# Gradient of single-query attention: the next pair's K scores moved ahead of its V transposes

## The chip, the cores and the metric

The kernel runs on one core of a Trainium2 chip. The metric is device time in microseconds (us); lower is better. The core has a TensorE (PE in the profile) for matmuls, a VectorE (DVE), a ScalarE (ACT), a GpSimd (POOL, used here only to set constants up) and a SyncE (SP), which here issues nearly all transfers between the main memory and the on-chip buffers. Each engine works its own instructions in order and waits on semaphores for the others.

## The reference

The forward pass is attention with one query per head over 8192 keys, 32 heads, 128 wide, in bf16; the outputs are its result and the gradients with respect to q, k and v for a given gradient of the output.

```python
B, H, Sq, Skv, Dh = 1, 32, 1, 8192, 128
def _fwd_reference(q, k, v):
    scale = q.shape[-1] ** -0.5
    scores = jnp.einsum('bhqd,bhkd->bhqk', q, k) * scale
    attn = _softmax(scores, axis=-1)
    return jnp.einsum('bhqk,bhkd->bhqd', attn, v)
_out, _vjp = jax.vjp(_f, q, k, v)
_grads = _vjp(grad_out)
return (_out0, *grads)          # out, dq, dk, dv
```

Per head this is: s = K q, p = softmax(scale s), out = V^T p, dp = V do, ds = scale p (dp - sum(p dp)), dq = K^T ds, dk = ds q^T, dv = p do^T. K and V are read once (134 MB), dk and dv, of the same size, are written once; all else is small.

## The kernel before

**Tiles.** Two heads make a pair; there are 16 pairs (HP). K and V of a pair are tiles of 128 partitions by 128 rows by 128 columns, 4 MB each. There are three K buffers and two V buffers, taken from pools whose tiles go round: a load of pair t takes the buffer that K of pair t-3, or V of pair t-2, leaves. dK is written into K's own buffer and dV into V's, eight blocks of 16 rows each, and stored from there; so a buffer is free for its next load when its store has landed.

**Steps of a pair t**, by function:
- `k_block(t, c)`, c from 0 to 7: VectorE transposes a block of K in 32x32 squares (L184, tile XK_sb, three buffers); TensorE multiplies it by a window on q (four matmuls, L192) into the bank s_ps.
- `s_back`, `s_top`, `s_exp`, `s_sum`, `p_of`: the softmax. VectorE turns s_ps back (L199) and takes the maximum (L204), TensorE turns it over partitions (L207), VectorE reduces (L214), ScalarE takes the exponential (L217), TensorE sums (L222), VectorE inverts (L233), ScalarE writes p (L235) and the window win_p (L228).
- `v_bank(t, m)` and `v_copy(t, m)`, m from 0 to 15: TensorE transposes four squares of V into one of three PSUM banks (L249), ScalarE copies the bank to XV_sb (L255). `v_scores(t, z)` multiplies four such banks by do (L266) into dp_ps. A bank can be refilled only after its copy.
- `contract(t, "p")`: out from V, 32 matmuls (L305); `contract(t, "ds")`: dq from K, 32 matmuls. `gather`, every fourth pair, brings their sums out (L312, L317, L319).
- `v_back`, `pd_sum`, `ds_of`: VectorE turns dp back (L276), the products' sum goes over TensorE (L285), VectorE makes ds (L290, L292, L295), ScalarE the window win_ds.
- `outer(t, "p", r)` and `outer(t, "ds", r)`, r from 0 to 7: VectorE writes dV over V and dK over K, a block at a time (L325). `store` issues the transfer on SP (L335), `load` the loads (L80).

**Order.** It is written out by hand (`tc.manual_schedule`), one list for all engines; each engine takes its own instructions in the order of that list. The body for pair t holds also the dK blocks of the pair before, o = t-1, in pieces (`dk(a, b)`). On VectorE the order is: eight K blocks of t, dK block 0 of o, the softmax of t between dK blocks 1 to 7, dpT, dV block 0, ds, dV blocks 1 to 7. On TensorE `early(t+1)`, which is banks 0 to 8 and score group 0 of the next pair's V, stands right behind `contract(t, "ds")` and `prepare(t+1)`, thus ahead of the next pair's K matmuls. ScalarE copies these nine banks while VectorE writes dV. On SP the order per pair is: store of dK of o (behind its block 7), store of dV of t, load of K of t+2, load of V of t+2. SP waits in that order, too: for VectorE before a store, for the old store's landing before a load.

**Beginning and end.** At the start K of pair 0 is loaded in quarters, then V(0), K(1), V(1), K(2). V(0)'s gradient is stored in quarters, and V(2) is then loaded in quarters. The last pair's dV and dK are stored in quarters, and dK of pair 14 in halves.

Of the kernel before, what the change touches and what calls it, by code (L numbers as in the profile page):

```python
# [11 lines left out]
BF16 = mybir.dt.bfloat16  # L12
# [3 lines left out]
NB = 8  # L16
# [6 lines left out]
K_BUFS = 3  # L23
V_BUFS = 2
# [3 lines left out]
def kernel(  # L28
# [12 lines left out]
    P = 128  # L41
    _, H, S, D = k.shape
    HP = H // 2
    NT = 2 * S // P
# [9 lines left out]


    consts = ctx.enter_context(tc.tile_pool(name="consts", bufs=1))
    kpool = ctx.enter_context(tc.tile_pool(name="kp", bufs=K_BUFS))
    vpool = ctx.enter_context(tc.tile_pool(name="vp", bufs=V_BUFS))
    xkpool = ctx.enter_context(tc.tile_pool(name="xkp", bufs=3))
    xvpool = ctx.enter_context(tc.tile_pool(name="xvp", bufs=2))  # L60
    backs = ctx.enter_context(tc.tile_pool(name="backs", bufs=2))
# [6 lines left out]
    psQ = ctx.enter_context(tc.tile_pool(name="psQ", bufs=1, space=PSUM))  # L68
    psM = ctx.enter_context(tc.tile_pool(name="psM", bufs=1, space=PSUM))

    Kt, Vt, st, acc = {}, {}, {}, {}

    def rows_of(x, t, a, b):
        return x[0, 2 * t:2 * t + 2].rearrange("h s d -> (h s) d").rearrange("(p n) d -> p n d", p=P)[:, a:b, :]

    def load(x, X, t, pool, tag, parts):
        X[t] = pool.tile([P, NT, D], BF16, tag=tag, name=tag + "t")
        L = NT // parts
        for c in range(parts):
            nc.sync.dma_start(X[t][:, c * L:(c + 1) * L, :], rows_of(x, t, c * L, (c + 1) * L))  # L80

    def load_k(t, parts=1):
        load(k, Kt, t, kpool, "K", parts)

    def load_v(t, parts=1):
        load(v, Vt, t, vpool, "V", parts)

    rows = consts.tile([H, 2, D], BF16)
    nc.sync.dma_start(rows[:, 0, :], q.rearrange("b h s d -> (b h s) d"))
# [1 line left out]
    load_k(0, 4)  # L91
    load_v(0)
    load_k(1)
    load_v(1)
    load_k(2)

    ident = consts.tile([P, P], BF16)
# [74 lines left out]
    def weights_q(t):  # L172
        nc.scalar.copy(q_win[:].rearrange("p c (a j) -> p c a j", j=SL)[:, :, 0:P // SL, SL - 1].rearrange(  # L173
            "p c (a j) -> p c a j", a=NQ)[:, :, :, 0], q_blk[:, t])

    def weights_do(t):
        for z in range(2):
            nc.scalar.copy(do_win[z * W:(z + 1) * W, :, :, SL - 2 + z].rearrange("p s e -> p e s"),
                           do_cols[z * W:(z + 1) * W, :, 2 * t:2 * t + 2])

    def k_block(t, c):
        x = st[t]
        X = xkpool.tile([P, BN, NW, QD], F32, tag="XK", name="XK_sb")
        nc.vector.transpose(X[:], Kt[t][:, c * BN:(c + 1) * BN, :].rearrange("p n d -> p (n d)").bitcast(F32).rearrange(  # L184
            "p (n w j) -> p n w j", n=BN, w=NW))
        if c == 0:
            x["s"] = psS.tile([P, 512], F32, tag="s", name="s_ps")
        cols = X[:].rearrange("p n w i -> p (n w i)").bitcast(BF16).rearrange(
            "p (n w i e) -> p w e n i", n=BN, w=NW, e=2)
        for w in range(NW):  # L190
            for e2 in range(2):
                nc.tensor.matmul(x["s"][:], lhsT=q_win[:, 2 * w + e2, SL - 1 - c:SL - 1 - c + P],  # L192
                                 rhs=cols[:, w, e2], start=(c == 0 and w == 0 and e2 == 0),
                                 stop=(c == NB - 1 and w == NW - 1 and e2 == 1), skip_group_check=True)

    def s_back(t):
        x = st[t]
        x["sT"] = backs.tile([P, BN, QD], F32, tag="back", name="sT")
        nc.vector.transpose(x["sT"][:].rearrange("p n r -> p (n r)"), x.pop("s")[:])  # L199
# [21 lines left out]
    def s_sum(t, rs):  # L221
        nc.tensor.matmul(st[t]["m"][:, 0:1], lhsT=same[:], rhs=rs[:], start=True, stop=True, skip_group_check=True)  # L222
# [17 lines left out]
    def v_bank(t, m):  # L240
        x = st[t]
        z, i = divmod(m, NM // TB)
        if i == 0:
            x["XV", z] = xvpool.tile([P, NM, P], F32, tag="XV", name="XV_sb")
        T_ps = psT.tile([P, TB, P], F32, tag="T", name="T_ps")
        words = Vt[t][:].rearrange("p n d -> p (n d)").bitcast(F32)
        for j in range(TB):
            at = (i * TB + j) * NZ + z
            nc.tensor.transpose(T_ps[:, j, :], words[:, at * P:(at + 1) * P], ident_f[:])  # L249
        x["T", m] = T_ps  # L250

    def v_copy(t, m):
        x = st[t]
        z, i = divmod(m, NM // TB)
        nc.scalar.copy(x["XV", z][:, i * TB:(i + 1) * TB, :], x.pop(("T", m))[:])  # L255

    def v_scores(t, z):
        x = st[t]
        cols = x.pop(("XV", z))[:].rearrange("p m s -> p (m s)").bitcast(BF16).rearrange(
            "p (m s e) -> p e m s", s=P, e=2)  # L260
        if z == 0:
            x["dp"] = psD.tile([P, 512], F32, tag="dp", name="dp_ps")
        at = SL - 2 - 2 * z
        for e2 in range(2):
            for b in range(NQ):
                nc.tensor.matmul(x["dp"][b * QD:(b + 1) * QD, :], lhsT=do_win[:, b // 2, e2, at:at + QD],  # L266
                                 rhs=cols[:, e2, :, b * QD:(b + 1) * QD],
                                 start=(z == 0 and e2 == 0), stop=(z == NZ - 1 and e2 == 1), skip_group_check=True)
# [62 lines left out]
    def store(t, which, parts=1, last=None):  # L331
        X, dst = (Kt[t], out_2) if which == "ds" else (Vt[t], out_3)
        L = NT // parts
        for c in (range(parts) if last is None else (last,)):
            nc.sync.dma_start(rows_of(dst, t, c * L, (c + 1) * L), X[:, c * L:(c + 1) * L, :])  # L335
# [9 lines left out]

    NV = NZ * NM // TB

    EARLY = 9

    def early(t):  # L350
        for m in range(EARLY):
            v_bank(t, m)
            v_copy(t, m)
            if m == 5:
                v_scores(t, 0)

    q_columns()
    do_columns()
    prepare(0)
    weights_q(0)  # L360
    weights_do(0)
    for t in range(HP + 1):
        o = t - 1
        now, old = t < HP, t > 0

        parts = 4 if o == HP - 1 else 2 if o == HP - 2 else 1

        def dk(a, b):
            for r in range(a, b if old else a):
                outer(o, "ds", r)  # L370
                if (r + 1) % (NB // parts) == 0:
                    store(o, "ds", parts, r * parts // NB)

        if now:
            for c in range(NB):
                k_block(t, c)
            if t + 1 < HP:
                weights_q(t + 1)
        dk(0, 1)
        if now:  # L380
            if old:
                v_scores(t, 1)
                v_bank(t, 9)
                v_copy(t, 9)
            s_back(t)
            s_top(t)
        dk(1, 2)
        if now:
            rs = s_exp(t)
            if old:  # L390
                for m in (10, 11, 12):
                    v_bank(t, m)
            s_sum(t, rs)
            if old:
                v_copy(t, 10)
                v_copy(t, 11)
        dk(2, 3)
        if now:
            p_of(t)
            if old:  # L400
                v_copy(t, 12)
                v_bank(t, 13)
                v_copy(t, 13)
                contract(t, "p")
                v_bank(t, 14)
                v_copy(t, 14)
                v_scores(t, 2)
                v_bank(t, 15)
                v_copy(t, 15)
                v_scores(t, 3)  # L410
            else:
                for m in range(NV):
                    v_bank(t, m)
                    v_copy(t, m)
                    if m == 7:
                        contract(t, "p")
                    if m % 4 == 1 and m > 1:
                        v_scores(t, m // 4 - 1)
                v_scores(t, 3)
            if t + 1 < HP:  # L420
                weights_do(t + 1)
        dk(3, NB)
        if not now:
            break
        v_back(t)
        pd_sum(t)
        if t % ST == ST - 1:
            gather(t, "p")
        if t % ST == 0 and old:
            gather(o, "ds")  # L430
        outer(t, "p", 0)
        ds_of(t)
        contract(t, "ds")
        if t + 1 < HP:
            prepare(t + 1)
            early(t + 1)
        else:
            gather(t, "ds")
            result(o_all, out_0)
            result(dq_all, out_1)  # L440
        fine = t == 0 or t == HP - 1
        for r in range(1, NB):
            outer(t, "p", r)
            if fine and r % 2:
                store(t, "p", 4, r // 2)
        if not fine:
            store(t, "p")
        if 0 < t and t + 2 < HP:
            load_k(t + 2)
        if t + 2 < HP:  # L450
            load_v(t + 2, 4 if t == 0 else 1)
# [32 lines left out]
```

## Time and profile before

| | |
|---|---|
| Time, median of 3 runs | 648.37 us (647.52 to 649.14) |
| The profiled execution: its time | 647.27 us |
| its span, first to last instruction | 645.5 us |
| TensorE matmuls busy | 445.6 us (69%) |
| VectorE busy | 505.0 us (78%) |
| ScalarE busy | 203.8 us (32%) |
| Moved by DMA | 268.97 MB, mean 417 GB/s |
| Mean granted TensorE clock | 0.831 |
| VectorE waits for the K matmuls (L184, on s_ps) | 82.0 us |
| TensorE waits for V loads (L249) | 80.3 us in 14 waits |
| ScalarE waits for V transposes (L255) | 179.0 us |

Busy time is the time in which an engine had an instruction under way; waiting, and the issuing of transfers, is not counted. A wait is put down to what ended it. Transfers are in flight long after they were issued: the page gives 19.4 us from issue to landing for a V tile of 4 MB and 23.8 us for the store of a dK tile. Busy shares are means over the whole span; what holds the end up must be read stage by stage.

### The profile page before, as it was taken

What the parts mean: (1) busy time and instruction counts of PE and PEld (TensorE: products, weight loads), DVE (VectorE), ACT (ScalarE), POOL (GpSimd) and SP (SyncE); (2) the same over time, 40 slices, a digit from 0 to 9 for tenths busy, and PEclk for the clock granted to TensorE, in tenths of its full rate; (3) what the DMA queues carried; (4) which work ended last, traced back from release to release, by engine and by line L of the source; (5) the groups of instructions that cost most, each with busy time, mean ns of one, the idle gap of its engine ahead of it and who ended that gap; (6) DMA issues with size and microseconds to landing.
All of it is one profiled execution on the core that took longest, in us unless ns stands there. A gap on an engine that the chain in (4) does not pass through costs nothing.

```text
span 645.5 us, 7988 instructions
## 1 busy us (share of the span) xinstructions
PE 445.6 (69%) x3256; PEld 252.8 (39%) x3256; DVE 505.0 (78%) x608; ACT 203.8 (32%) x456; POOL 4.4 (1%) x10
## 2 busy tenths in 40 slices
PE   5678795585967758577684965849667586765860
PEld 2444342443535334254442634425353342533430
DVE  8169899498796888858789696986959878597885
ACT  1443333332343323134232333313334142342320
POOL 2000000000000000000000000000000000000000
PEclk9789798686887869878698887869869696796985
DMA  8998999999999999999999999999999999999589
GB/s 358 446 429 330 354 421 435 434 425 437 429 429 428 434 428 425 432 437 423 432 437 429 430 434 427 429 441 427 423 439 424 420 434 422 438 422 423 249 376 374
DMA packets 11748, 268.97 MB, mean 417 GB/s; under 512 B 1472, under 2 KB 1472, under 8 KB 1472
## 3 DMA queue, kind: packets, MB, share of 16 engines
q1 hardware_dynamic: 11568, 268.45, 97.6%
q8 instruction: 25, 0.41, 0.2%
q14 instruction: 11, 0.09, 0.0%
q10 hardware_dynamic: 144, 0.02, 0.0%
HBM read 134.23 MB, written 134.23 MB: 416 GB/s over the span
## 4 chain that ended last, share of the span: by engine, by line
DMA 46%; DVE 24%; PE 18%; issue 5%; ACT 4%; SPq 0%; DVEq 0%; ACTq 0%
DMA Vt<-in_v_dram 25%; DMA out_dram<-Vt 22%; DVE Vt L325 12%; PE T_ps L249 10%; DVE XK_sb L184 4%; PE acc_p L305 4%; DVE Kt L325 3%; PE dp_ps L266 2%; ACT XV_sb L255 2%; DVE dpT L276 1%; PE s_ps L192 1%; ACT p_rep L235 1%; DVE sT L199 1%; ACT win_p L228 1%; PE m_ps L317 1%
## 5 line engine op out<-in xcount | busy, mean ns | idle before, releaser
L249 PE MATMUL T_ps<-ident_f,Vt 128*128 128x128 f32 x1024 | 167.6, 322 | 81.4 <-DMA Vt<-in_v_dram 80.3
L184 DVE STREAM_TRANSPOSE XK_sb<-Kt 128x1024 f32<-128x1024 f32 x128 | 147.6, 1210 | 82.2 <-PE s_ps L192 82.0
L255 ACT COPY XV_sb<-T_ps 128x512 f32<-128x512 f32 x256 | 141.0, 588 | 179.7 <-PE T_ps L249 179.0
L249 PEld LDWEIGHTS T_ps<-ident_f,Vt 128*128 128x128 f32 x1024 | 141.3, 167 | 118.0 <-issue 96.8
L325 DVE TENSOR_TENSOR Kt<-ds_rep,qd 128x2048 bf16<-128x2048 bf16 x128 | 149.9, 1214 | 0.5
L325 DVE TENSOR_TENSOR Vt<-p_rep,qd 128x2048 bf16<-128x2048 bf16 x128 | 148.0, 1217 | 0.0
L192 PE MATMUL s_ps<-XK_sb,q_win 128*128 128x512 bf16 x512 | 124.7, 382 | 7.2 <-DVE XK_sb L184 2.0
L192 PEld LDWEIGHTS <-q_win 128*128 128x128 bf16 x512 | 49.7, 97 | 76.4 <-issue 23.9
L305 PE MATMUL acc_ds<-Kt,win_ds 128*32 128x512 bf16 x512 | 53.2, 590 | 26.4 <-ACT win_ds L228 26.4
L305 PE MATMUL acc_p<-Vt,win_p 128*32 128x512 bf16 x512 | 40.2, 469 | 19.3 <-ACT win_p L228 19.3
L266 PE MATMUL dp_ps<-XV_sb,do_win 128*32 128x512 bf16 x512 | 40.7, 393 | 10.8 <-ACT XV_sb L255 10.8
L276 DVE STREAM_TRANSPOSE dpT<-dp_ps 128x512 f32<-128x512 f32 x16 | 11.5, 717 | 36.9 <-PE dp_ps L266 36.9
L173 ACT COPY q_win<-q_blk 128x16 bf16<-128x16 bf16 x16 | 4.3, 267 | 111.5 <-PE s_ps L192 111.1
L305 PEld LDWEIGHTS <-win_ds 128*32 128x32 bf16 x512 | 17.4, 132 | 50.3 <-ACT win_ds L228 25.8
L305 PEld LDWEIGHTS <-win_p 128*32 128x32 bf16 x512 | 14.2, 110 | 37.9 <-ACT win_p L228 22.8
L170 ACT CAST qd<-m_ps 128x256 bf16<-128x256 f32 x16 | 6.0, 372 | 55.9 <-PE m_ps L166 55.7
L285 PE MATMUL m_ps<-pd,same 128*128 128x1 f32 x32 | 6.5, 273 | 19.4 <-DVE m_ps L279 19.4
L266 PEld LDWEIGHTS <-do_win 128*32 128x32 bf16 x512 | 9.3, 95 | 26.8 <-issue 26.8
L228 ACT COPY win_ds<-ds 64x128 bf16<-64x128 bf16 x32 | 9.5, 296 | 24.9 <-DVE ds L292 24.7
L285 PEld LDWEIGHTS m_ps<-pd,same 128*128 128x128 f32 x32 | 5.2, 203 | 27.3 <-DVE m_ps L279 27.3
L217 ACT ACTIVATE e<-sT,nbias 128x128 f32<-128x128 f32 x16 | 8.2, 512 | 17.5 <-DVE nbias L214 17.5
L199 DVE STREAM_TRANSPOSE sT<-s_ps 128x512 f32<-128x512 f32 x16 | 11.5, 717 | 1.4 <-PE s_ps L192 1.1
(59 smaller groups left out, 141.5 us busy)
## 6 DMA issues: line engine op xcount, KB each, us to landing
Vt<-in_v_dram SPq DMA_DIRECT2D x15, 4096.0 KB, 19.4
Kt<-in_k_dram SPq DMA_DIRECT2D x15, 4096.0 KB, 19.6
out_dram<-Kt SPq DMA_DIRECT2D x14, 4096.0 KB, 23.8
out_dram<-Vt SPq DMA_DIRECT2D x14, 4096.0 KB, 21.5
out_dram<-Vt SPq DMA_DIRECT2D x8, 1024.0 KB, 9.9
Kt<-in_k_dram SPq DMA_DIRECT2D x4, 1024.0 KB, 7.9
Vt<-in_v_dram SPq DMA_DIRECT2D x4, 1024.0 KB, 8.9
out_dram<-Kt SPq DMA_DIRECT2D x2, 2048.0 KB, 8.4
```

What stands on the lines that cost most here:

```text
L184: nc.vector.transpose(X[:], Kt[t][:, c * BN:(c + 1) * BN, :].rearrange("p n d -> p (n d)").bitcast(F32).rearrange("p (n w j) -> p n w j", ...
L192: nc.tensor.matmul(x["s"][:], lhsT=q_win[:, 2 * w + e2, SL - 1 - c:SL - 1 - c + P], rhs=cols[:, w, e2], start=(c == 0 and w == 0 and e2 == 0),
L199: nc.vector.transpose(x["sT"][:].rearrange("p n r -> p (n r)"), x.pop("s")[:])
L217: nc.scalar.activation(e[:].rearrange("p (c n) -> p n c", c=NB), x["sT"][:, :, 0:NB], ACT.Exp, bias=nbias[:], scale=scale, accum_out=rs[:])
L228: nc.scalar.copy(win[which][a:b, :, at + 4 * s:at + 4 * s + 4], src[a:b].rearrange("p (g j) -> p g j", j=4))
L249: nc.tensor.transpose(T_ps[:, j, :], words[:, at * P:(at + 1) * P], ident_f[:])
L255: nc.scalar.copy(x["XV", z][:, i * TB:(i + 1) * TB, :], x.pop(("T", m))[:])
L266: nc.tensor.matmul(x["dp"][b * QD:(b + 1) * QD, :], lhsT=do_win[:, b // 2, e2, at:at + QD], rhs=cols[:, e2, :, b * QD:(b + 1) * QD], start ...
L276: nc.vector.transpose(dpT[:].rearrange("p m r -> p (m r)"), x.pop("dp")[:])
L285: nc.tensor.matmul(x["m"][:, 1:2], lhsT=same[:], rhs=x["pd"][:], start=True, stop=True, skip_group_check=True)
L305: nc.tensor.matmul(acc[which][b * QD:(b + 1) * QD, :], lhsT=win[which][:, g, at:at + QD], rhs=X[:, 4 * g:4 * g + 4, :].rearrange("p n d -> ...
L325: nc.vector.tensor_tensor(X[:, a:b, :].rearrange("p n (a b) -> p n a b", b=R), x[which][:, a:b, :].unsqueeze(2).to_broadcast([P, BN, D // ...
```

## The change

K and V live in fixed buffers (three and two named tiles) instead of pool tiles, used in the same turn; a load waits for what touched the same part of the buffer. The K blocks of pair t+1 move from the start of body t+1 into body t: blocks 0 to 3 stand between dV blocks 3 to 7 of pair t, block 4 behind the last one, and blocks 5, 6 and 7 behind the store of dV, each followed by one V bank of t+1 (0 to 2). Then the window on q for pair t+2 is set. `early` is gone: banks 3 to 15 and the four score groups of a pair stand in its own body, between the dK blocks and the softmax. The K blocks of pair 0 are in the prologue. Loads and stores are the same, in the same order on SP.

```diff
@@ -54,8 +54,6 @@
 
 
     consts = ctx.enter_context(tc.tile_pool(name="consts", bufs=1))
-    kpool = ctx.enter_context(tc.tile_pool(name="kp", bufs=K_BUFS))
-    vpool = ctx.enter_context(tc.tile_pool(name="vp", bufs=V_BUFS))
     xkpool = ctx.enter_context(tc.tile_pool(name="xkp", bufs=3))
     xvpool = ctx.enter_context(tc.tile_pool(name="xvp", bufs=2))
     backs = ctx.enter_context(tc.tile_pool(name="backs", bufs=2))
@@ -68,22 +66,25 @@
     psQ = ctx.enter_context(tc.tile_pool(name="psQ", bufs=1, space=PSUM))
     psM = ctx.enter_context(tc.tile_pool(name="psM", bufs=1, space=PSUM))
 
-    Kt, Vt, st, acc = {}, {}, {}, {}
+    st, acc = {}, {}
+    k_in = [consts.tile([P, NT, D], BF16, name=f"K{i}") for i in range(K_BUFS)]
+    v_in = [consts.tile([P, NT, D], BF16, name=f"V{i}") for i in range(V_BUFS)]
+    Kt = {t: k_in[t % K_BUFS] for t in range(HP)}
+    Vt = {t: v_in[t % V_BUFS] for t in range(HP)}
 
     def rows_of(x, t, a, b):
         return x[0, 2 * t:2 * t + 2].rearrange("h s d -> (h s) d").rearrange("(p n) d -> p n d", p=P)[:, a:b, :]
 
-    def load(x, X, t, pool, tag, parts):
-        X[t] = pool.tile([P, NT, D], BF16, tag=tag, name=tag + "t")
+    def load(x, X, t, parts):
         L = NT // parts
         for c in range(parts):
             nc.sync.dma_start(X[t][:, c * L:(c + 1) * L, :], rows_of(x, t, c * L, (c + 1) * L))
 
     def load_k(t, parts=1):
-        load(k, Kt, t, kpool, "K", parts)
+        load(k, Kt, t, parts)
 
     def load_v(t, parts=1):
-        load(v, Vt, t, vpool, "V", parts)
+        load(v, Vt, t, parts)
 
     rows = consts.tile([H, 2, D], BF16)
     nc.sync.dma_start(rows[:, 0, :], q.rearrange("b h s d -> (b h s) d"))
@@ -345,24 +346,23 @@
 
     NV = NZ * NM // TB
 
-    EARLY = 9
-
-    def early(t):
-        for m in range(EARLY):
-            v_bank(t, m)
-            v_copy(t, m)
-            if m == 5:
-                v_scores(t, 0)
+    def v_part(t, m):
+        v_bank(t, m)
+        v_copy(t, m)
+
+    HALF = NB // 2
 
     q_columns()
     do_columns()
     prepare(0)
     weights_q(0)
     weights_do(0)
+    for c in range(NB):
+        k_block(0, c)
+    weights_q(1)
     for t in range(HP + 1):
         o = t - 1
         now, old = t < HP, t > 0
-
         parts = 4 if o == HP - 1 else 2 if o == HP - 2 else 1
 
         def dk(a, b):
@@ -371,47 +371,45 @@
                 if (r + 1) % (NB // parts) == 0:
                     store(o, "ds", parts, r * parts // NB)
 
-        if now:
-            for c in range(NB):
-                k_block(t, c)
-            if t + 1 < HP:
-                weights_q(t + 1)
-        dk(0, 1)
+        dk(0, 2)
         if now:
             if old:
-                v_scores(t, 1)
-                v_bank(t, 9)
-                v_copy(t, 9)
+                v_part(t, 3)
+                v_part(t, 4)
             s_back(t)
             s_top(t)
-        dk(1, 2)
+            if old:
+                v_scores(t, 0)
+                v_part(t, 5)
+                v_part(t, 6)
+        dk(2, 3)
         if now:
             rs = s_exp(t)
             if old:
-                for m in (10, 11, 12):
+                for m in (7, 8, 9):
                     v_bank(t, m)
             s_sum(t, rs)
             if old:
-                v_copy(t, 10)
-                v_copy(t, 11)
-        dk(2, 3)
+                v_copy(t, 7)
+                v_copy(t, 8)
+        dk(3, 4)
         if now:
             p_of(t)
             if old:
-                v_copy(t, 12)
-                v_bank(t, 13)
-                v_copy(t, 13)
+                v_copy(t, 9)
+                v_scores(t, 1)
+                v_part(t, 10)
+                v_part(t, 11)
                 contract(t, "p")
-                v_bank(t, 14)
-                v_copy(t, 14)
+                v_part(t, 12)
+                v_part(t, 13)
                 v_scores(t, 2)
-                v_bank(t, 15)
-                v_copy(t, 15)
+                v_part(t, 14)
+                v_part(t, 15)
                 v_scores(t, 3)
             else:
                 for m in range(NV):
-                    v_bank(t, m)
-                    v_copy(t, m)
+                    v_part(t, m)
                     if m == 7:
                         contract(t, "p")
                     if m % 4 == 1 and m > 1:
@@ -419,7 +417,7 @@
                 v_scores(t, 3)
             if t + 1 < HP:
                 weights_do(t + 1)
-        dk(3, NB)
+        dk(4, NB)
         if not now:
             break
         v_back(t)
@@ -433,7 +431,6 @@
         contract(t, "ds")
         if t + 1 < HP:
             prepare(t + 1)
-            early(t + 1)
         else:
             gather(t, "ds")
             result(o_all, out_0)
@@ -443,8 +440,16 @@
             outer(t, "p", r)
             if fine and r % 2:
                 store(t, "p", 4, r // 2)
+            if t + 1 < HP and r >= HALF - 1:
+                k_block(t + 1, r - HALF + 1)
         if not fine:
             store(t, "p")
+        if t + 1 < HP:
+            for c in range(HALF + 1, NB):
+                k_block(t + 1, c)
+                v_part(t + 1, c - HALF - 1)
+            if t + 2 < HP:
+                weights_q(t + 2)
         if 0 < t and t + 2 < HP:
             load_k(t + 2)
         if t + 2 < HP:
```

## The prediction

> **What bounds the kernel now.** I read first the sliced page (who is busy when), then long windows of the DMA engines, then the order of issues on SP, then VectorE's timeline in the first pairs. The page's DMA rows:
>
> ```profile
> DMA  8998999999999999999999999999999999999589
> GB/s 358 446 429 330 354 421 435 434 425 437 429 429 428 434 428 425 432 437 423 432 437 429 430 434 427 429 441 427 423 439 424 420 434 422 438 422 423 249 376 374
> q1 hardware_dynamic: 11568, 268.45, 97.6%
> ```
>
> The transfers fill the span except in slices 3 to 4 (48 to 81 us) and 37 (597 to 613 us). The windows (busy time of each engine, clock, DMA share, GB/s) say it closer:
>
> ```profile
> 90.00:590.00 500.00, 349.22 (x2571) 198.46 (x2569) 400.30 (x477) 158.58 (x354) 0.00 (x0) 0.83 1.00 430
> ...
> 62.00:64.00 2.00, 1.52 (x12) 1.04 (x9) 1.82 (x6) 1.52 (x5) 0.00 (x0) 1.00 0.18 74
> 64.00:66.00 2.00, 0.73 (x13) 0.33 (x16) 2.00 (x3) 1.93 (x5) 0.00 (x0) 0.98 0.02 8
> ...
> 608.00:610.00 2.00, 1.52 (x12) 1.13 (x10) 1.84 (x5) 1.45 (x4) 0.00 (x0) 1.00 0.08 33
> 610.00:612.00 2.00, 0.74 (x14) 0.33 (x16) 1.98 (x3) 1.92 (x5) 0.00 (x0) 1.00 0.00 0
> ```
>
> From 90 to 590 us the DMA share is 1.00 at 430 GB/s: no order of the compute can win there, only lose. What can be won are two holes, at 62 to 66 and near 604 to 612 us. The issues on SP show how the transfers queue:
>
> ```profile
> 69.93 0.34 SPq L335 DMA_DIRECT2D out_dram<-Kt  x1
> 83.03 0.34 SPq L335 DMA_DIRECT2D out_dram<-Vt  x1
> 90.22 0.34 SPq L80 DMA_DIRECT2D Kt<-in_k_dram  x1
> 99.91 0.34 SPq L80 DMA_DIRECT2D Vt<-in_v_dram  x1
> ...
> 611.47 4.88 SPq L335 DMA_DIRECT2D out_dram<-Kt  x2
> 622.87 7.14 SPq L335 DMA_DIRECT2D out_dram<-Vt  x4
> ```
>
> The K load at 90.22 waited for K(0)'s store to land, the V load at 99.91 for V(1)'s store: 9.69 us apart, which is one 4 MB tile at 430 GB/s (4.19/0.430 = 9.75). The landings in the trace follow one another by 9.65 to 10.05 us through the span (a few by 10.4 to 11.4): one line, served in order of issue, 9.7 us for a tile, 2.45 to 2.5 us for a quarter. So the time is the sum of transfers plus the moments in which the line is empty. Per pair it is four tiles, 39.3 us (V loads land at 119.95 and 591.28, twelve pairs apart). VectorE has 505.0/16 = 31.6 us of work per pair.
>
> An empty line also costs a start. The page lists K(14)'s two 2 MB stores with 8.4 us to landing, the first of them issued into an empty line, where 2 MB move in 4.85: about 3.4 us. The first quarter of V(2), issued at 65.21 into an empty line, landed at 71.03, 5.8 where 2.5 is the transfer: again 3.4.
>
> VectorE at the first pairs:
>
> ```profile
> 38.44 0.72 DVE L276 STREAM_TRANSPOSE dpT<-dp_ps 128x512 f32<-128x512 f32 x1 [17.34 <-PE dp_ps L266]
> 41.46 8.03 DVE L325 TENSOR_TENSOR Vt<-p_rep,qd 128x2048 bf16<-128x2048 bf16 x7
> 49.41 9.12 DVE L184 STREAM_TRANSPOSE XK_sb<-Kt 128x1024 f32<-128x1024 f32 x8
> 71.95 0.72 DVE L276 STREAM_TRANSPOSE dpT<-dp_ps 128x512 f32<-128x512 f32 x1 [2.05 <-PE dp_ps L266]
> 74.97 8.03 DVE L325 TENSOR_TENSOR Vt<-p_rep,qd 128x2048 bf16<-128x2048 bf16 x7
> ```
>
> A product block (L325) is 8.03/7 = 1.147 us, a K block (L184) 9.12/8 = 1.14, and without a wait for V a pair takes 33.5 us from one dpT to the next (the following one, 71.95 to 103.83, 31.9).
>
> **The change, part by part.** Nothing is removed: 8 K blocks, 16 V banks and 16 product blocks per pair stay, and no DMA is added.
>
> *Quarter release of V(0).* In the changed instruction order each quarter load of V(2) waits for its own quarter's store; before, the first waited for all four (landings 57.8, 60.2, 62.7, 65.1). Back to back the loads would land at 67.6, 70.1, 72.5, 75.0 instead of 71.0, 73.5, 76.0, 80.4 (3.4 us start, and a fourth quarter of 4.4). Quarters 2 and 3 are stored later now (2 and 4 K blocks ahead of them: 47.25+2.3 and 49.52+4.6 = 54.1), still ahead of their turn. Worth up to 5.4 us, if something follows. Elsewhere a tile is loaded whole and waits for one store as before: the fixed buffers cost and give nothing.
>
> *K blocks ahead of the V store.* K blocks 0 to 3 of the next pair (4 x 1.14 = 4.6 us) now stand before the last dV block, and with it before the store of V on SP; behind that store in SP's queue stand the K load, the V load and the dK store.
>
> *V transposes later.* Nine banks and one score group, which ran on TensorE and ScalarE under the dV blocks, now follow the K blocks. Listing the changed order for pair 1 with durations from rows (K block 1.14, product 1.147, four K matmuls 7.91/8 = 0.99, bank 1.53/3 = 0.51, ScalarE copy 0.55, score group 0.58, p contraction 2.5 = 40.2/16, from 0.47 and 0.59 for the softmax steps): the last K block ends on VectorE at 58.0 (before 58.5), its matmuls at 59.7; banks 2 to 4 to 61.3; the maximum's transpose 61.75; exp 64.5 behind the copies of banks 5 and 6; p and its window 67.0 behind copies 7 and 8; contraction to 69.5; banks 12 to 15 with their copies to 72.8; last scores 73.4. dpT at 73.5 instead of 71.95, with dK done at 70.4: a wait of 3.1 us where 2.05 stood. Then 1.1 + 1.15 + 0.9, seven dV and four K blocks (8.0 + 4.6): V(1)'s store is issued at 89.3. The same listing of the old order gives 81.6 where 83.03 was, so I add 1.4: 90.7. Bounds: 86.2 if the V stage never delays dpT (70.4 + 15.8), 94 if its 13 late banks take 0.76 each (4.54 us for 24 transposes right after a wait for V) and the contraction 3.1.
>
> *What the line does with it.* K(0)'s store is issued near 70.5 as before, now behind loads that end at 75.0, and lands at 84.7 (before 90.2). Then the line is empty until V(1)'s store at 90.7: landed at 90.7 + 3.4 + 9.7 = 103.8, before 99.85. So the 5.4 us won are lost again in a new hole 6 us wide plus its start: **+4.0 us** for every later landing (86.2: -0.5; 94: +7.3).
>
> *Steady pairs.* A compute cycle in the listing is 73.5 - 38.4 = 35.1, say 36, against 39.3 of the line; it was 32.7. So it stays hidden with 3 us to spare. VectorE's wait of 82.0 us for K score matmuls should go: TensorE no longer stands before an unlanded V there. In its place K(t+1) is wanted some 9 us earlier, and its load lands one tile (9.7) before V(t+1): a wait of L184 for the K load. Behind it on VectorE stand the dV blocks and thus the V store: K landed + 4 x (1.14 + 1.147) = 9.2 us, some 0.5 us before V(t+1) lands. Its turn comes after the dK store, 9.7 us after V landed: 10 us to spare. **0 us**.
>
> *The end.* Let V(15) land at L (before 591.28). Stores of K(13) and V(14) end at L + 20.0 (611.3). K(14)'s first half came at L + 20.2 (611.47) into an empty line. Now the K scores are nearly done at L: last K block L + 4.1, dK blocks 3 and 7 6.2 and 12.4 us behind it by the listing, so the halves are issued at L + 10 and L + 17, in time. dpT at L + 20 to 21 (before 26.7), first dV quarter 4.85 later as before (618.02 to 622.87), L + 26, while K(14) ends at L + 29.7; eight quarters of 2.48, last issued 15.9 after the first, never late. L + 49.6 + 1.1, before L + 54.2: **-3.6 us**, the hole at 611. Bounds: 0 if the store stays late, -3.6 at most, since then the line is full.
>
> Sum: 4.0 - 3.6 = +0.4 us on a span of 645.5; 647.3 + 0.4 = 647.7 for the profiled execution, which lies 1.1 us under the median 648.4: **648.8 us**.
>
> **A rule on TensorE's clock.** Granted clock in the rows: 24 transposes at 591.4 to 595.9 take 4.54 us mostly at 0.50, 12 at 596.4 take 1.53 at 1.00, and 12 right behind K matmuls (60.1 to 62.6) 1.47. The Trainium skill, "TensorE: Matmul & The Clock Gate" (What's actually happening), says that the clock is halved after an idle window of about 3.4 us and restored after a busy one. The trace agrees for the wait on V; whether K matmuls half the time are busy enough no row shows. By this rule the late banks could start slow, which is the second rival.
>
> **The rivals.**
> 1. *The hole at 85 us is larger or smaller.* Each us of V(1)'s issue is one us of the total. Larger, at 92.5 to 95: 650.5 to 653. For it: three engines hand over in turn in the moved stage, and my listing was 1.4 short once. Chance 0.24. Smaller, at 86.2 to 88: 644.2 to 646.0, the gain of both holes. For it: VectorE has only 31.6 us of work. Against: ScalarE has 14 copies and the softmax in line behind the last K block. Chance 0.18.
> 2. *The V stage bounds every pair* (slower). Place: between the last K block and dpT, where nothing but dK blocks (9.2 us) covers 13 banks. If they take 0.76 instead of 0.51 and the contraction 3.1, the cycle is 36 + 3.3 + 0.6, and 0.7 for the gathers, 40.6; from 39.3 on it decides; 1.3 us in some 13 pairs is +17, with the hole at 94 about 670; with half of the banks slow only the gather pairs lose, about 655. Against: banks right behind K matmuls ran at 0.49. Chance 0.16.
> 3. *The change does not do what it says:* the V wait keeps VectorE idle because the maximum's transpose stands behind bank 4 on TensorE. In the first pairs V has landed, so it can only keep the hole at 611: 652.4, counted within the first rival.
>
> **How the numbers follow.** Forecast 0.42, hole larger 0.24, smaller 0.18, V stage 0.16. With 0.3% (2 us) as what can be told from no change: faster 0.18, same 0.42, slower 0.40. Range: below, halfway into the smaller hole, 645; above, halfway between the mild and the full V stage, 659. The forecast's own range is 646.4 to 650.4.
>
> **What would show it.** DMA share near 1 at 62 to 66 us, near 0 at about 85 to 92; V(1)'s store issued at 90 to 91; L184 waiting for the K load instead of s_ps (82.0 us), small waits of L249 for V; 39.3 us between V loads in the middle; no hole at 611. I am wrong if V(1)'s store comes before 88 or after 93, if V loads stand over 39.5 us apart, or if the first K(14) half is issued after the line ran empty.

## The result, and the profile after

The changed kernel takes 651.42 us (median of 5 runs, 650.04 to 651.71) where the one before takes 648.37 (647.52 to 649.14): a ratio of 1.0046, 95% interval 1.0031 to 1.0061. It is slower by 3 us, inside the stated range and 2.6 us above the forecast; the likeliest case (within 0.3%) was missed, the case slower was given 0.40. The profiled execution is one of 651.42 us, its span 649.6 against 645.5.

The page of the changed kernel, the rows that answer to those of before:

```profile
DMA  8999959999999999999999999999999999999986
GB/s 360 447 420 394 424 220 390 419 439 422 437 431 428 435 426 436 428 426 437 429 429 432 427 435 428 425 430 435 417 436 423 429 424 419 426 419 421 422 373 266
q1 hardware_dynamic: 11568, 268.45, 97.3%
```

The hole of slices 3 and 4 (330 and 354 GB/s before) is filled, and a new one stands in slice 5, 220 GB/s; slice 37, 249 before, is full. Windows of the changed kernel (busy time of PE, PEld, DVE, ACT, POOL, then clock, DMA share, GB/s):

```profile
90.00:590.00 500.00, 353.69 (x2621) 187.65 (x2620) 397.01 (x475) 156.42 (x363) 0.00 (x0) 0.82 1.00 427
...
62.00:64.00 2.00, 1.82 (x18) 1.05 (x16) 1.93 (x5) 1.76 (x4) 0.00 (x0) 1.00 0.98 414
64.00:66.00 2.00, 2.00 (x22) 1.89 (x19) 1.62 (x4) 1.30 (x4) 0.00 (x0) 1.00 1.04 438
...
82.00:84.00 2.00, 1.87 (x4) 0.55 (x4) 2.00 (x3) 0.06 (x1) 0.00 (x0) 0.50 0.12 49
84.00:86.00 2.00, 1.67 (x4) 0.55 (x4) 2.00 (x3) 0.00 (x0) 0.00 (x0) 0.50 0.00 0
86.00:88.00 2.00, 1.60 (x5) 0.54 (x4) 2.00 (x3) 0.00 (x0) 0.00 (x0) 0.50 0.00 0
88.00:90.00 2.00, 1.60 (x5) 0.39 (x3) 2.00 (x3) 0.00 (x0) 0.00 (x0) 0.51 0.00 0
...
610.00:612.00 2.00, 1.87 (x28) 1.28 (x28) 2.00 (x2) 1.93 (x5) 0.00 (x0) 1.00 0.96 410
```

From 82 us on the transfers run dry (a DMA share of 0.12), and from 84 to 90 us nothing is transferred, while VectorE is busy all the time: it does the work that the next store waits for. The issues on SP and VectorE's timeline around it:

```profile
71.80 0.34 SPq L336 DMA_DIRECT2D out_dram<-K  x1
89.94 0.34 SPq L336 DMA_DIRECT2D out_dram<-V  x1
90.38 0.38 SPq L81 DMA_DIRECT2D K<-in_k_dram  x1
102.06 0.34 SPq L81 DMA_DIRECT2D V<-in_v_dram  x1
```

```profile
74.36 0.72 DVE L277 STREAM_TRANSPOSE dpT<-dp_ps 128x512 f32<-128x512 f32 x1 [2.59 <-PE dp_ps L267]
...
80.78 1.24 DVE L185 STREAM_TRANSPOSE XK_sb<-K 128x1024 f32<-128x1024 f32 x1
81.94 1.18 DVE L326 TENSOR_TENSOR V<-p_rep,qd 128x2048 bf16<-128x2048 bf16 x1
...
88.73 1.18 DVE L326 TENSOR_TENSOR V<-p_rep,qd 128x2048 bf16<-128x2048 bf16 x1
```

K(0)'s store, issued at 71.80, landed at 84.65. V(1)'s store came only at 89.94, 6.9 us later than before: dpT was 2.4 us later (74.36, before 71.95), and four K blocks stand ahead of the store. It landed at 102.0 (the V load at 102.06 waited for it). The waits:

```profile
DVE dpT L277 <- PE dp_ps L267: 56.1, 16, 17.2
DVE XK_sb L185 <- DMA K<-in_k_dram: 48.3, 12, 5.0
```

VectorE's wait for the K matmuls, 82.0 us before, is gone; in its place it waits 48.3 us, in 12 waits, for the K load. The moments at which SP issues the V loads, each being the landing of the V store two pairs earlier, give the pace of the steady pairs. Of the changed kernel:

```profile
499.66 0.34 SPq L81 DMA_DIRECT2D V<-in_v_dram  x1
...
539.29 0.34 SPq L81 DMA_DIRECT2D V<-in_v_dram  x1
...
579.06 0.34 SPq L81 DMA_DIRECT2D V<-in_v_dram  x1
```

and of the kernel before:

```profile
492.96 0.34 SPq L80 DMA_DIRECT2D Vt<-in_v_dram  x1
...
532.43 0.34 SPq L80 DMA_DIRECT2D Vt<-in_v_dram  x1
...
571.87 0.34 SPq L80 DMA_DIRECT2D Vt<-in_v_dram  x1
```

39.63 and 39.77 us a pair now, 39.47 and 39.44 before. From V(3)'s landing to V(15)'s, twelve pairs, it is 39.54 against 39.28. One profile of each kernel is read here. The 4.1 us between the two profiled spans lie as follows: V(3) lands at 124.0 instead of 120.0 (+4.0), V(15) at 598.4 instead of 591.3 (a further +3.2 in the steady pairs), and from there to the end 51.2 instead of 54.2 (-3.0).

### The profile page after: what moved, and what is told of

It is laid out like the page before. It is cut to its first block, busy times and chain, and to the rows that moved or that the text cites. A ratio compares the mean times of both kernels' runs of the same rounds, so it can differ in the third digit from the quotient of the medians.

```text
span 649.6 us, 8002 instructions
## 1 busy us (share of the span) xinstructions
PE 448.7 (69%) x3256; PEld 238.2 (37%) x3256; DVE 503.6 (78%) x608; ACT 196.4 (30%) x456; POOL 4.4 (1%) x10
## 4 chain that ended last, share of the span: by engine, by line
DMA 41%; DVE 28%; PE 14%; issue 11%; ACT 4%; SPq 0%; DVEq 0%
DMA K<-in_k_dram 34%; DVE XK_sb L185 17%; PE T_ps L250 6%; DVE K L326 5%; DMA out_dram<-K 4%; DVE V L326 3%; PE s_ps L193 3%; DMA V<-in_v_dram 3%; ACT XV_sb L256 3%; PE dp_ps L267 2%; PE acc_p L306 1%; DVE sT L200 1%; PE m_ps L208 0%; ACT p_rep L236 0%; DVE mx L205 0%
## 5 line engine op out<-in xcount | busy, mean ns | idle before, releaser
L193 PE MATMUL s_ps<-XK_sb,q_win 128*128 128x512 bf16 x512 | 173.4, 476 | 101.4 <-DVE XK_sb L185 100.4
L185 DVE STREAM_TRANSPOSE XK_sb<-K 128x1024 f32<-128x1024 f32 x128 | 152.6, 1223 | 48.5 <-DMA K<-in_k_dram 48.3
L326 DVE TENSOR_TENSOR V<-p_rep,qd 128x2048 bf16<-128x2048 bf16 x128 | 150.9, 1202 | 0.0
L326 DVE TENSOR_TENSOR K<-ds_rep,qd 128x2048 bf16<-128x2048 bf16 x128 | 150.0, 1215 | 0.5
L250 PE MATMUL T_ps<-ident_f,V 128*128 128x128 f32 x1024 | 137.7, 281 | 2.5 <-DMA V<-in_v_dram 2.5
L250 PEld LDWEIGHTS T_ps<-ident_f,V 128*128 128x128 f32 x1024 | 116.1, 143 | 41.8 <-issue 10.7
L193 PEld LDWEIGHTS <-q_win 128*128 128x128 bf16 x512 | 57.9, 113 | 200.0 <-issue 175.3
L306 PE MATMUL acc_ds<-K,win_ds 128*32 128x512 bf16 x512 | 55.5, 611 | 26.1 <-ACT win_ds L229 26.1
L277 DVE STREAM_TRANSPOSE dpT<-dp_ps 128x512 f32<-128x512 f32 x16 | 11.5, 717 | 56.1 <-PE dp_ps L267 56.1
L306 PE MATMUL acc_p<-V,win_p 128*32 128x512 bf16 x512 | 30.6, 380 | 1.9
L236 ACT ACTIVATE p_rep<-e,rinv 128x512 bf16<-128x512 f32 x16 | 12.0, 747 | 0.7 <-DVE rinv L234 0.7
## 6 DMA issues: line engine op xcount, KB each, us to landing
out_dram<-V SPq DMA_DIRECT2D x8, 1024.0 KB, 10.4
```

What stands on the lines that cost most here:

```text
L236: nc.scalar.activation(x["p"][:], x["e"][:].unsqueeze(2).to_broadcast([P, NT, R]), ACT.Copy, scale=rinv[:])
L277: nc.vector.transpose(dpT[:].rearrange("p m r -> p (m r)"), x.pop("dp")[:])
L306: nc.tensor.matmul(acc[which][b * QD:(b + 1) * QD, :], lhsT=win[which][:, g, at:at + QD], rhs=X[:, 4 * g:4 * g + 4, :].rearrange("p n d -> ...
L326: nc.vector.tensor_tensor(X[:, a:b, :].rearrange("p n (a b) -> p n a b", b=R), x[which][:, a:b, :].unsqueeze(2).to_broadcast([P, BN, D // ...
```

## The experiments

To mix the orders I wrote both into one body, chosen for each pair by `t in AHEAD`: where it holds, the pair's K blocks and V banks stand as in the changed kernel, else as before. The changed kernel is `AHEAD = range(1, HP)`. The kernel before, run again beside each group, had medians of 648.1 to 648.9; the ratios are to those. The table has the medians and, from one profile each, V(1)'s store (issue of its first part, landing of the whole), the landing of V(3), the pace of the twelve pairs to V(15), and the time from V(15)'s landing to the end, in us.

```
kernel                               median   V(1) store      V(3)    pace    end
before                               648.37   83.0 ->  99.8   120.0   39.28   54.2
changed                              651.42   89.9 -> 102.0   124.0   39.54   51.2
e1 fixed buffers, old order          643.08   82.5 ->  95.9   116.8   39.27   54.6
e2 pools, new order                  651.88   88.6 -> 100.7   123.0   39.60   51.2
e3 new order for pair 15 alone       641.07   82.8 ->  96.5   117.3   39.24   51.2
e4 new order from pair 3             643.64   81.6 ->  95.0   115.9   39.52   51.1
e5 changed, V(1) stored in quarters  646.17   78.7 ->  94.8   117.0   39.73   51.0
e6 e3, V(1) stored in quarters       638.26   75.2 ->  94.1   114.4   39.25   51.0
e7 e4, p contraction cut             640.95   79.9 ->  94.6   115.0   39.42   51.0
e8 e3, p contraction cut             638.80   80.0 ->  94.3   114.8   39.28   51.1
e9 K blocks behind the V store       646.43   83.4 ->  95.5   118.0   39.46   51.1
e10 V stores in halves               646.52   79.4 ->  95.7   118.5   39.53   51.1
e11 e4, a quarter of the transposes  638.93   80.3 ->  94.7   115.8   39.20   50.9
e12 e3, a quarter of the transposes  638.07   79.9 ->  94.0   114.3   39.11   52.8
```

**Which part costs: buffers or order.** Theory: the order costs, through the late V(1) store; rival A: fixed buffers or quarters cost. Four kernels.

e1, the buffers alone:

```diff
-    AHEAD = range(1, HP)
+    AHEAD = range(0)
```

> Fixed buffers and the quarter release as in the changed kernel, the order of the kernel before. Theory (the changed kernel loses at the start because V(1)'s store is issued late, at 89.9 us, into an empty line): V(2)'s quarters land back to back at about 75, K(0)'s store at 85, V(1)'s store is issued at 83 as before and lands at 94.5 instead of 99.85; nothing else moves, the hole before K(14)'s store stays 3.6 us. So 5.4 us under before: about 643. Rival A (fixed buffers or loads in quarters cost something themselves): at or above 648.4, and the changed kernel's loss is theirs.

Measured 643.08 us, ratio 0.9922 (0.9907 to 0.9937). V(2)'s quarters land at 74.5, V(1)'s store at 95.9. SP's issues:

```profile
69.44 0.34 SPq L336 DMA_DIRECT2D out_dram<-K  x1
82.55 0.34 SPq L336 DMA_DIRECT2D out_dram<-V  x1
84.31 0.34 SPq L81 DMA_DIRECT2D K<-in_k_dram  x1
95.97 0.34 SPq L81 DMA_DIRECT2D V<-in_v_dram  x1
```

The K load at 84.31 waited for K(0)'s store, so V(1)'s store, issued 1.8 us earlier, should have landed 9.7 later, at 94.0; it took 11.7. (The profile is of the longest of six runs, 644.53.) Rival A falls: the quarter release is worth 5 us where the V store follows in time.

e2, the order alone: the pools and the whole-tile release of the kernel before under the changed kernel's body.

```diff
+    kpool = ctx.enter_context(tc.tile_pool(name="kp", bufs=K_BUFS))
+    vpool = ctx.enter_context(tc.tile_pool(name="vp", bufs=V_BUFS))
...
+        X[t] = pool.tile([P, NT, D], BF16, tag=tag, name=tag + "t")
```

> Pools as before, the new order alone. Theory: V(2) lands at 80.4, K(0)'s store at 90.2, V(1)'s store is issued at 90 and lands at 100 to 102, so the late store costs about as much as in the changed kernel and the quarter release is worth nothing there: within 1 us of the changed kernel, 650.5 to 652.5. Rival A (fixed buffers cost): 3 us faster than the changed kernel, 648.4 or less.

Measured 651.88, ratio 1.0054 (1.0041 to 1.0067), as the changed kernel: under the new order the quarter release is worth nothing, and the loss is the order's.

e3 and e4, the new order at the end alone, and everywhere but at the start:

```diff
-    AHEAD = range(1, HP)
+    AHEAD = range(HP - 1, HP)    # e3
+    AHEAD = range(3, HP)         # e4
```

> Fixed buffers, the order of before for pairs 1 to 14, the new order for pair 15 alone. Theory: the 5.4 us at the start are kept, the hole before K(14)'s store closes (3.1 to 3.6 us), the middle runs as before (39.3 us per pair): 8.5 to 9 us under before, about 639.5. Rival B (the end gains only because the whole new order runs through): 643, as with fixed buffers alone.

> Fixed buffers, the order of before for pairs 1 and 2, the new order from pair 3 on. Theory in two parts: no hole at 85 us, the end's gain kept, so 639.5 if the middle costs nothing in the new order; if the new order itself slows the line by the 0.26 us per pair that one profile of each kernel shows (39.54 against 39.28), 3 us more than the kernel with only the last pair changed, about 642.5. Rival C (the new order bounds the pairs by compute): V loads over 39.8 us apart and 646 or more.

e3 measured 641.07, 0.9878 (0.9861 to 0.9896): the end shortens by 3.0 us with pair 15 alone in the new order, rival B falls. It lies 1.6 above what was expected; in its profile V(1)'s store landed at 96.5 instead of 94.5, the same 2 us as in e1. e4 measured 643.64, 0.9931 (0.9917 to 0.9944), 2.6 us above e3, with a pace of 39.52 against 39.24: the new order does slow the steady pairs, and the start has no part in that. Rival C falls too: the V loads stand less than 39.8 us apart.

**Is it the store, or the work before it?** e5 leaves the changed kernel's work as it is and lets V(1)'s store begin earlier:

```diff
-        fine = t == 0 or t == HP - 1
+        fine = t in (0, 1, HP - 1)
```

> The changed kernel with one edit: V(1)'s gradient is stored in quarters too, each behind its two dV blocks; all orders of work stay. Theory (the loss at the start is an empty line that waits for V(1)'s whole store): the quarters are issued from 78.5 to 90 us, K(0)'s store ends at 84.7, V(1)'s quarters land by 94.5 instead of 102.0, and every later landing is some 7.5 us earlier: 643.5 to 644.5, where the kernel with the old order for pairs 1 and 2 stood (643.6). Rival (the late K scores and V transposes of pair 1 themselves cost the time): 650 or more.

Measured 646.17, 0.9968 (0.9956 to 0.9981), 5.3 us under the changed kernel. Its issues:

```profile
71.84 0.34 SPq L336 DMA_DIRECT2D out_dram<-K  x1
78.66 11.65 SPq L336 DMA_DIRECT2D out_dram<-V  x4
90.42 0.37 SPq L81 DMA_DIRECT2D K<-in_k_dram  x1
94.84 0.34 SPq L81 DMA_DIRECT2D V<-in_v_dram  x1
```

The V load at 94.84 waited for the last quarter: 7.2 us earlier than in the changed kernel, with every K block and V bank still where it was. The rival falls as it was stated: most of what cost was the empty line. Something is left of it, though. From the landing of V(1)'s store, the loads of K(3) and V(3) took 22.0 to 22.8 us together in the five kernels whose pair 1 is in the new order (changed, e2, e5, e9, e10), against 20.1 to 21.1 in the other nine; so in the new order the transfers there are slower by some 2 us, one profile each. A further 2 us were lost later: the pace is 39.73 in this profile, the slowest of all, and why is open (V(3) landed 6.9 us earlier).

e6, the same edit in e3:

> The kernel with the new order for pair 15 alone, and V(1)'s gradient stored in quarters. Theory: there V(1)'s store was issued at 82.8, 2 us before K(0)'s store landed, and landed at 96.5, 2 us after back to back (94.5); quarters issued from 77 on close that: about 2 us less, 639. Rival (the 2 us are the store's own): unchanged, 641.

Measured 638.26 (638.12 to 638.57), 0.9845 (0.9831 to 0.9858), the fastest that computes everything. K(0)'s store landed at 84.37 and V(1)'s last quarter at 94.09, back to back. Its windows where the kernel before had its holes:

```profile
62.00:66.00 4.00, 2.59 (x22) 1.32 (x26) 3.86 (x6) 3.36 (x9) 0.00 (x0) 0.78 1.02 430
80.00:84.00 4.00, 3.76 (x33) 2.54 (x32) 4.00 (x4) 3.31 (x7) 0.00 (x0) 1.00 0.91 387
84.00:88.00 4.00, 3.64 (x16) 1.29 (x14) 4.00 (x5) 0.00 (x0) 0.00 (x0) 1.00 1.02 430
...
600.00:606.00 6.00, 5.81 (x71) 3.36 (x70) 4.99 (x6) 4.93 (x12) 0.00 (x0) 1.00 0.84 355
```

The transfers go on at 62 to 66 us, where the kernel before moved 8 to 74 GB/s, and through 80 to 88, where the changed kernel stood still; at the end the halves of K(14) follow without the pause of before.

**What slows the steady pairs.** By landings the V stores take the line 10.2 us in most pairs of the new order (9.7 to 10.0 before). e7 and e8 cut the p contraction, which the new order moves into that time; out is not computed in them.

```diff
-        for g in range(first, last):
+        few = [g for g in range(first, last) if which == "ds" or g < NQ or g >= NG - NQ]
+        for g in few:
```

> The kernel with the new order from pair 3 on; of the p contraction's 32 matmuls per pair only 8 are left, so out is not computed. Theory D (the new order puts the contraction, 1.9 us of 32 matmuls that read V, into the time of the V store, about 12.5 us after V's landing, and slows that transfer: 10.2 us against 9.7 to 10.0): V stores fall to 9.7 to 10.0, V loads stand 39.3 us apart instead of 39.5, 640.5 to 641. Rival E (the steady loss comes from something else, the moment at which SP issues the stores among it): 39.5 us, 643.5.

> The control: the same cut in the kernel with the old order for pairs 1 to 14; out is not computed. Theory D: here the contraction falls into the K load, whose transfers were 9.7 us; nothing to win, 39.2 to 39.3 us and 640.5 to 641. Rival E': taking 24 matmuls away speeds the line wherever they stand, 39.0 us and 638.

e7 measured 640.95, 0.9886 (0.9872 to 0.9899), e8 638.80, 0.9854 (0.9840 to 0.9867): 2.7 and 2.3 us less, nearly the same. In e8 that lies at the start (V(3) lands 2.5 us earlier, since V(1)'s store is issued earlier); in e7 0.9 us lie at the start and 1.1 in the twelve pairs. The pace moves from 39.52 to 39.42 and from 39.24 to 39.28, so the difference between the orders goes from 0.28 to 0.14. Theory D expected 39.3 and does not hold as the whole cause; whether the contraction has a part stays open, since the single profiles of the kernels in the new order that compute everything lie between 39.46 and 39.73. e7's total alone would have looked like theory D; the control takes that away.

e9 and e10 test whether the V store's late issue does it (0.4 to 1 us before the next V lands, behind the wait for the K load).

```diff
-            if t + 1 < HP and r >= HALF - 1:
-                k_block(t + 1, r - HALF + 1)
...
-            for c in range(HALF + 1, NB):
+            for c in range(NB):
                 k_block(t + 1, c)
-                v_part(t + 1, c - HALF - 1)
+                if c > HALF:
+                    v_part(t + 1, c - HALF - 1)
```

> The changed kernel with K blocks 0 to 3 behind the V store instead of between its dV blocks; K scores still stand ahead of the V transposes, V bank 0 to 2 behind K blocks 5 to 7. V(1)'s store is then issued at about 85.5 instead of 89.9 and lands at 97.6 instead of 102. Theory F (the steady 0.26 to 0.3 us per pair come from the V store that waits for the K load and is issued only 0.5 us before the next V lands): V stores fall from 10.2 to 9.7 to 10.0, V loads 39.3 us apart, about 643. Rival G (they come from the work of the V stage, all 16 banks, softmax and contraction, standing in the time of the V store): still 39.5, about 646.

For e10:

```diff
+            if not fine and r % 4 == 3:
+                store(t, "p", 2, r // 4)
...
-        if not fine:
-            store(t, "p")
```

> The changed kernel with every V store in two halves, behind dV blocks 3 and 7; the work of the engines keeps its order. V(1)'s first half is issued at about 80.8 and the second at 90, both land by 95: some 7 us less at the start than the changed kernel. Theory F (late issue of the V store): the steady pairs fall to 39.3 us as well, 641 to 642. Rival G (the work beside the store): 39.5 us and more, 644.5 to 646.

e9 measured 646.43, 0.9971 (0.9960 to 0.9983), e10 646.52, 0.9976 (0.9965 to 0.9987), at paces of 39.46 and 39.53; e9's profile is of the shortest of its eight runs, 644.41. In e9 the last whole V store was issued 12.9 us before V(15) landed, and the steady loss stayed. Theory F falls.

e11 and e12 leave one of each bank's four transposes and copy it four times; dq and dk are not computed.

```diff
-        for j in range(TB):
+        for j in range(1):
...
-        nc.scalar.copy(x["XV", z][:, i * TB:(i + 1) * TB, :], x.pop(("T", m))[:])
+        nc.scalar.copy(x["XV", z][:, i * TB:(i + 1) * TB, :], x.pop(("T", m))[:, 0:1, :].to_broadcast([P, TB, P]))
```

> The kernel with the new order from pair 3 on; of each V bank's four transposes one is left and ScalarE copies it four times, so dp, dq and dk are not the reference's. TensorE reads a quarter of V there. Theory G1 (TensorE's transposes of V, 64 in a row while K and V are being stored, slow the line): V loads 39.25 to 39.3 us apart instead of 39.5. Rival G2 (other work of the stage, or the place of the K blocks): 39.4 to 39.55. The total may fall by more than the pairs, since dpT of pair 1 and 2 comes earlier: V(3) is to be compared with V(15).

> The control: the same cut in the kernel with the old order for pairs 1 to 14. Theory G1: 39.2 to 39.27 us per pair as before (39.24), since there only nine banks stand in a row. If it falls by as much as the new order does, the transposes slow the line in both orders and do not explain the difference.

e11 measured 638.93, 0.9850 (0.9827 to 0.9874), e12 638.07, 0.9837 (0.9815 to 0.9858). The pace falls from 39.52 to 39.20 in the new order and from 39.24 to 39.11 in the old: the difference between the orders goes from 0.28 to 0.09 us, and that of the totals from 2.6 to 0.9. So with three quarters of the transposes gone the line is faster in both orders, and more so in the new one; by the pace about two thirds of the steady loss go with them. By another count it is half: of the 32 KB packets between 100 and 590 us, 199 took over 1.3 us in e4 and 108 in e3, and 137 in e11 and 90 in e12. These are single profiles.

It is not shown that a transpose slows the transfers that run beside it, and the packets speak against it. In the changed kernel, of the packets that overlap a V transpose by over 0.3 us in their first 1.21 us, 32 of 2089 took over 1.3 us; of the others, 174 of 4283. What grew most are the slow packets beside K blocks on VectorE: 13 of 1679 before, 97 of 1998 now, still 82 of 2124 in e11, and 87 of 1748 in e9, where the K blocks do not alternate with dV blocks. Standing beside is not yet a cause, and no run takes the K blocks away. So the loss belongs to the new order of the work; by what path it reaches the transfers stays open.

## Why the prediction held, and where it failed

**Quarter release:** V(2)'s last quarter landed at 74.9 (75.0 foretold).

**V(1)'s store late, a new hole:** issued at 89.9 (90.7), after dpT at 74.4 (74.9 with the 1.4 us I had added); the hole was seen, and e1 and e5 show that it is mostly the store's lateness that costs. The +4.0 us for later landings came out by luck, since errors cancel: the store was issued 0.8 us earlier than foretold, the start of the empty line cost 2.4 us and not 3.4 (12.06 from issue to landing, less 9.7), and the next two loads took 11.1 and 10.8 us instead of 9.7 and 10.4.

**The end:** -3.0 for -3.6; K(14)'s first half was issued at 608.56, 10.1 us behind V(15) (10 foretold). e3 shows it from pair 15 alone. Of the missing 0.6 us, 0.3 are the stores of K(13) and V(14), 20.3 us instead of 20.0, and 0.4 that of K(14), 10.1 instead of 9.7. The line was full by its landings alone: from 645 to 648 us the DMA share is 0.08 to 0.06, about one engine of sixteen, and the last landing is at 648.6. The pause before 611 us was of that kind, too (a share of 0.08 from 608 to 610), so it is longer than the 3.6 us that closing it could give.

**Steady pairs, "0 us": the step that failed.** I had shown that compute stays hidden behind the line and that each store is issued in time, and both held: VectorE waits for the K load, and the DMA share is 1.00. But I took 9.7 us per tile as given. The line itself ran at 39.54 us a pair instead of 39.28, so that V loads stood over 39.5 us apart, which I had named as a sign of being wrong; twelve pairs of 0.26 are 3.2 us, and with them the sum is 4.0 + 3.2 - 3.0 = 4.2, as the spans differ (4.1). e4 against e3 ties it to the order of the work; e11 and e12 make half to two thirds of it go with three quarters of the V transposes, and how is open.

**The rivals.** The V stage did not become the bound: dpT waited 56.1 us in 16 waits, 17.2 of them in pair 0, but the pairs were paced by the line. Its premise, late banks at half the clock, did not hold either: the clock was 0.50 from 84 to 90 us and 1.00 from 90 on, ahead of the banks, and a transpose averaged 281 ns against 322 before. The Trainium skill, "TensorE: Matmul & The Clock Gate" (What's actually happening), lets a busy window of about 3.4 us restore the clock. The trace shows that in part: the clock rose, but only after some 6 us in which TensorE was busy 1.6 to 1.7 of each 2 us. What the half clock did slow are the K matmuls, four in each 2.26 us between dV blocks: 476 ns on average against 382, hidden. That the V wait would keep the hole at 611 did not happen.

## What to carry to other kernels

When the transfers fill the span, ask of a reordering first when each store reaches the queue: work put ahead of a store is paid nearly in full in the first pairs, where the line still runs empty (e1 to the changed kernel: V(1)'s store 7.4 us later, V(3) 7.1), and later the lateness of the store cost nothing here (e9, e10). A transfer that becomes free earlier is worth something only if the next one is ready; here the quarter release was worth 5 us under the old order and nothing under the new. And a full line is not a constant: check the time of one tile in the profile after, even if its share of busy time stays at 1.00, and run the control before a cut is taken for the cause.

## What the hardware showed that was not expected

- A store issued 1.8 to 2.0 us before the landing of the one ahead of it (e1, e3) still landed 11.7 us after that, 2 more than back to back. By then the line was all but empty: the DMA share was 0.31 from 81 to 82 us in both, and 0.15 and 0.08 from 82 to 83, so a last few engines set the landing. One issued 5 us ahead (e7: 79.88, K(0) landed at 84.94) took its 9.65 after the one before it.
- Single packets of 32 KB take 1.21 us on a DMA engine. Between 100 and 590 us, 110 of them took over 1.3 us in the kernel before and 206 in the changed one; 87 to 110 in the old order (before, e1, e3, e6) and 184 to 251 in the new (changed, e2, e4, e5, e9). The share of busy time, 1.00 in both, does not show it.
- In the old order (before, e1, e3, e6) stores take about 10.0 us from about pair 8 on and mostly 9.7 ahead of it; loads mostly take 9.7 in both halves. Why was not tried.
- With TensorE busy 1.6 to 1.7 of each 2 us by the matmul records (84 to 90 us), the granted clock stayed at 0.50, and rose at 90.
